# Two-layer attention and bilinear GLU on one core: two more groups' scores in block form, and every queue in a new order

## The chip, the cores and the metric

One core of one Trainium2 chip runs the whole program in one launch. The metric is the time of an execution on the device in microseconds (us), the median of several runs. Before the change it is 383.03 us, the median of three runs (381.39, 383.03, 383.17).

## The reference

Input x has 2048 tokens of 448 values. Two layers alternate, A (attention with a dilated local window) and B (a gated product without a nonlinearity), each with a layer norm ahead and a residual, and the pair runs twice with the same weights:

```python
def _A_ref(x, wqkv, wo):          # H = 16 heads of Dh = 28; W, dil = 8, 2
    q, k, v = split(x @ wqkv)
    idx = pos[:, None] - (jnp.arange(8) * 2)[None, :]     # 8 keys: 0, 2, .. 14 back
    logits = einsum("bhsd,bhswd->bhsw", q, k[idx]) * Dh ** -0.5, -1e9 where idx < 0
    o = einsum("bhsw,bhswd->bhsd", softmax(logits), v[idx])
    return o @ wo

def _B_ref(x, w_gate, w_up, w_down):                      # F = 1792
    return ((x @ w_gate) * (x @ w_up)) @ w_down

x = x + _A_ref(_layernorm(x), wqkv, wo)
x = x + _B_ref(_layernorm(x), w_gate, w_up, w_down)
# and both once more
```

## The kernel before

**Stages.** The program calls the four layers 0 to 3 (0 and 2 attention, 1 and 3 GLU). Tokens are cut into chunks (`ACH`, `BCH`, lines 54 and 55): layer 0 into 256, 512, 512, 512, 256, so that chunk 4 is tokens 1792 to 2047. `SEQ` (line 67) interleaves chunks of different layers: A00 A01 B10 A02 B11 and so on. A block is 128 tokens.

**Layer norm and transposes.** `ln_chunk` (line 619) makes statistics and the normalized rows of a block on DVE (line 650) and turns them: for the first 14 blocks of layer 0 on PE (line 660, copied out at 668), for all others with a DMA transpose in SP's queue (line 653), into `xnTa` for layers 0 and 2 and `xnTb` for 1 and 3.

**Attention.** `qk_chunk` (line 745) makes K and Q of a chunk, four units of four heads, evicted to `qk` at line 778. `v_group` (line 800) makes V. Queries are handled in groups of two blocks of 120 (group 0 has one block of 128), 9 groups in a layer. A block of 120 queries and 128 keys is cut into two halves c of 64 queries and 64 keys. There are two forms of scores:

- the old form in `attn_front` (line 894): for each head a matmul of 28 rows (head dimension) by 64 keys by 64 queries, 64 of them for a group (line 908), four PSUM banks, then exponential (915) and mask `MK` (925);
- the block form in `attn_front2` (line 933): two heads share 64 rows, and K is copied into `KB` with the other head's rows set to zero, four masked copies for a group (lines 957, 958, on POOL, DVE or ACT by the order), so that one matmul of 64 rows by 128 columns gives both heads; 16 of them for each c (line 965), two banks, exponential (971), mask `MB` (980). V's halves then stand swapped for half of the heads, so that V is evicted in three pieces (`new_way` in `v_group`, line 867) where the old form has one (888) beside the piece for the last four heads (844).

`new_way` chooses: the block form for layer 2 and for groups from `G0` = 4 on in layer 0. `KB` lies in columns of `qk` that hold no K at that time (`kb_col`, line 730; layer 0 puts it over the keys of early tokens and waits for all of their readers, `old_readers`). `attn_back` (986) multiplies with V (line 998, "AV": 64 small matmuls for a group), `norm` divides by the sums, and `y_blocks` (1048) makes the output projection Y of two blocks, added to x at 1061.

**GLU.** `b_chunk` (1071) makes gate and up of 128 features in one unit of 14 matmuls (G), evicts gate on ACT (1097), multiplies on DVE (1100) into `hT[:, fc, hs, :]`, where hs alternates with the chunk, and then multiplies with w_down (Dd). The first chunk uses hs = 0, the second hs = 1; before that parts of `hT` hold staged weights and masks: `MT2`, from which `MB` is made, is in `hT[:, 10, 1]`, a zero tile for warm-up matmuls in `hT[:, 13, 1]`.

**Order.** Each operation is added to a list and has a number; nothing is ordered at run time. `ORD` (line 59) writes out, engine by engine, the order of all numbers, and `BANK` the PSUM banks of each PE operation. Both come from a planner that is not in the file, with assumed durations. `a+b@24.40` in PE's order interleaves a burst of small matmuls a with steps of a large operation b, cut into strips of 32 columns (line 371); b is then a's host. Each engine works its list strictly in order and waits on semaphores for what an operation needs; SP's list holds nearly all DMAs, so that a DMA that waits holds up those behind it. Weight loads wait in SP's queue for an earlier weight's landing (`link`).

Of the kernel before, what the change touches and what calls it, by code (L numbers as in the profile page):

```python
# [44 lines left out]
G0 = 4  # L45
# [14 lines left out]
    "pe": "72!v 73 74 75 76 77 78 79 80 81 82 83 138!v 142!v 84 85 86 87 88 89 227!a 229 228!p 231!o 230!p 232!p 233 161!v 239!d 158!a 234!p 240!p 164!v 268!a 167!a 269!p 260!a 243!a 261!p 262!a 256!a 191!a 263!p 258!a 257!p 206!v 259!p 182!a 188!a 185!v 248!v 276!a 370!a 368!v 212!a 371!p 215!a 369!p 374!v 586!d 209!a 375!p 281!v 584!a 587 585!p 588!a 582!v 272!a 583!p 589 273!p 372!v 293!v 373!p 387!a 289!a 388!p 290!p 396!a 511!a 298!v 513!a 512!p 514!p 509!a 415!o 401!a 420!a 510!p 515!a 391!v 516!p 392!p 528!a 306!v 529!p 329!d 307!p 540!a 323!v 326!v 545!a 335!v 320!v 341!a 332!v 347!a 353!a 338!v 409!a 344!a 548+410@23.25.40!v 601!a 350!v 359!v 602!p 356!a 362!d 423!v 363!v 562!a 533!v 364!p 534!p 365 567!a 458!d 464!v 455!a 556!a 431!v 618!v 557!p 432!p 570+467~4@24.40!av 461!v 479!a 473!a 613!v 485!v 470!a 476!a 482!v 488!a 494!v 491!v 497!a 640!v 635!a 498!v 606!a 499!p 500 578!v 503 579!p 504 607 621+505@24.40.40!p 506 675!a 643+681~4@24.40!vv 678!v 772!d 751!v 773!p 752!p 749!a 755!v 750!p 629!a 753!a 630!p 754!p 756 690!a 768!a 687!a 651!v 769!p 652!p 684!a 702!v 779!a 696!v 693!v 699!a 708!v 714!a 802!o 711!a 784!v 705!a 717!a 723!a 718!v 787!d 797 719!p 720 805+724~2@24.40.40!-v 837!v 725!p 726 846!v 843!v 840!v 917!d 915!a 918!p 911!v 913!v 916!p 914!p 930!a 912 931!p 935!a 813!v 936!p 814!p 942!v 849 969!a 852!v 964!v 858!a 855!a 861!a 947!v 870!v 864!a 873!v 867!a 950+876@24.40!a 997!d 879!a 1003!v 972+880~2@24.40!va 1000!a 881!p 882 885!v 994!v 886 1015!v 1012!v 887!p 1009!v 1006 888 958!v 1024 1018!v 959!p 1122!v 1126!v 1123!p 1127!p 1141!v 1146 980!a 1142!p 981!p 1147 1124!a 1030!v 1125!p 1128!v 1021!a 1058!v 1129!p 1052!a 1027!v 1055!a 1033!v 1153!a 1061!v 1064!a 1067!a 1070!a 1036!a 1079!v 1073!v 1076!a 1037 1082!a 1158!a 1038!p 1180!v 1091!a 1039 1088 1085!a 1094!a 1161+1224~1@24.40!vd 1215!v 1095 1175!v 1096!p 1097 1183+1218~1@24.40!vv 1221!v 1329!v 1169!v 1299!v 1170!p 1300!p 1297!a 1293!v 1312!v 1295!a 1298!p 1313!p 1294 1296!p 1317!v 1191!a 1318!p 1236!v 1192!p 1334!o 1227!a 1230!v 1356!o 1233!v 1239!v 1248!a 1351!o 1242!v 1245!v 1254!a 1378!v 1251!v 1337+1265@24.24.40.40!v 1322!v 1266 1373!a 1323!p 1267!p 1257!v 1359+1258@24.40!v 1345!v 1259!p 1346!p 1381+1260~3@24.40!-v 1268 1413!v 1422!v 1419!a 1416!v 1367!v 1425!v 1368!p 1428!v 1389!a 1434!v 1390!p 1440!v 1437!v 1431!v 1452!a 1449!a 1446!v 1443!v 1463!a 1497!d 1455!v 1509!v 1464 1456 1465!p 1491!v 1466 1457!p 1500!a 1503!v 1512 1458 1521!a 1494!v 1559!a 1524!a 1562!v 1515!v 1574!a 1506!v 1527!a 1571!a 1518!v 1565!a 1530!a 1583!v 1568 1577 1580!v 1595!a 1533!v 1586!a 1592!v 1534 1541!a 1535!p 1542 1589!v 1543!p 1598!v 1536 1544 1601!v 1607 1604!v",  # L60
    "act": "2 3 14 131 132 135 136 140 144 149 235 150 236 155 237 156 162 159 238 165 168 241 179 242 270 180 271 245 244 173 266 197 221 174 198 222 192 267 264 265 186 203 204 278 277 377 376 379 282 592 253 254 286 287 274 275 294 378 295 389 390 397 398 314 300 315 299 518 519 416 303 304 421 520 393 406 330 541 324 327 546 336 407 342 439 321 348 440 354 333 339 345 549 351 550 360 445 446 357 603 425 563 428 553 429 554 459 568 465 456 619 571 462 572 468 659 733 734 480 660 474 665 666 614 575 486 477 471 483 495 489 492 641 636 576 739 740 608 623 622 676 644 682 645 821 626 679 627 758 774 648 649 757 759 760 782 827 822 828 895 691 688 685 703 697 780 700 896 694 709 803 988 712 715 785 706 798 806 901 902 989 838 847 792 844 841 1106 1107 810 811 793 922 920 932 943 970 965 850 859 853 856 862 948 1046 865 1047 871 874 951 868 877 952 998 1004 974 1001 1112 995 1016 1113 1013 955 956 1010 1007 1025 977 1019 978 1130 1132 1148 1031 1131 1199 1205 1200 1022 1059 1277 1206 1133 1053 1278 1028 1056 1034 1154 1062 1065 1068 1071 1080 1074 1077 1083 1159 1092 1181 1089 1086 1283 1284 1225 1176 1216 1166 1167 1184 1185 1219 1330 1222 1188 1304 1189 1314 1301 1332 1397 1319 1335 1237 1228 1398 1231 1357 1403 1404 1234 1240 1352 1372 1243 1249 1246 1255 1252 1379 1338 1342 1343 1374 1361 1360 1364 1382 1414 1365 1475 1386 1476 1423 1420 1387 1417 1426 1429 1435 1481 1482 1441 1432 1438 1447 1450 1453 1444 1553 1554 1498 1510 1492 1504 1501 1522 1513 1495 1525 1560 1516 1563 1575 1507 1528 1572 1519 1566 1531 1569 1578 1584 1596 1581 1593 1587 1599 1590 1606",
# [36 lines left out]
def n_grp():  # L98
    return 9 if PAIRED else NQB
# [304 lines left out]
def build(nc, A_x, A_wqkv, A_wo, B_w_gate, B_w_up, B_w_down, out):  # L404
# [325 lines left out]
    def kb_col(li, g):  # L730
        return (HALF if li else 0) + 512 * (g % 2)
# [9 lines left out]
    def block_readers(a, z):  # L741

        return [("S2", 0, g, c) for g in range(G0, n_grp()) if kb_col(0, g) < z and kb_col(0, g) + 512 > a for c in range(2)]

# [55 lines left out]
    def v_group(li, qbs, prio):  # L800
# [32 lines left out]
        if plain:  # L833
            while n == 2 and rpos["v2"] % NV2 == NV2 - 1:
                rpos["v2"] += 1
            r2 = [ring("v2", ("AV", li, q)) for q in qbs]
            t0 = [r[0] for r in r2]
            assert n == 1 or t0[1] == t0[0] + 1
            v2slot.update({(li, q): t for q, t in zip(qbs, t0)})
            def fp(E):  # L840
                dst = v2_sb[0:nk, t0[0]:t0[0] + n, :].rearrange("p s (h e) -> p s h e", e=32)[:, :, :, 0:DH]
                src = ps[0:nk, bk[1]:bk[1] + 1, VD - nv:D - nv] if split else ps[0:nk, bk[0]:bk[0] + 2, VD:D]
                src = src.rearrange("p s (h e) -> p s h e", e=DH)
                return E.activation(dst, src, ACT.Copy) if hasattr(E, "activation") else E.tensor_copy(dst, src)
            sc.add(("act", "dve"), one(fp, [("VT", li, q) for q in qbs]), {"act": act_est(n * (D - VD)), "dve": dve_est(n * (D - VD))},
                   deps=list(keys) + ["c_v2"] + [r[1] for r in r2], prio=prio)
# [396 lines left out]
```

## Time and profile before

| | |
|---|---|
| median of three runs | 383.03 us |
| the profiled execution | 384.27 us |
| its span, first to last instruction | 382.5 us |
| granted TensorE clock | 1.00 |
| masked copies of K (lines 957, 958) | 3 on ACT, 4 on DVE, 51 on POOL |
| old scores, matmuls (line 908) | 224 |
| block scores, matmuls (line 965) | 432 |

In profile lines PE is the matrix engine, PEld its weight loads (beside the matmuls), DVE the vector engine, ACT the scalar engine, POOL GpSimd, SP the engine whose queue issues DMAs (SPq). A line such as `29.73 0.50 PE L368 ... x6 [1.82 <-DMA a<-b]` gives the start, the length, engine and source line, and in brackets the idle time before and what ended it. Most matmuls go through one helper, so they all have line 368, and tiles tell them apart: `xnTa,WQK` K and Q, `WV,xnTa` V, `wo_g,oT` Y, `xnTb,WGU` gate and up, `WD,hT` the down product. A timeline row that stands for one instruction ends when its result is out; the next starts earlier, so that lengths overlap and the distance of starts is the cost.

### The profile page before, as it was taken

The page shows a single profiled execution, that of the slowest core. Times are in us where ns is not written, and L with a number is a line of the kernel's source. Part 1 is how long each engine was busy: PE and PEld are TensorE (multiplying, and loading weights), DVE is VectorE, ACT ScalarE, POOL GpSimd, SP SyncE. Part 2 cuts the span into 40 slices and gives each one's busy share as a digit, 9 for nine tenths or more (in the row PEclk, how much of TensorE's full clock was granted, in tenths as well). Part 3 has the DMA queues.
Part 4 walks back from the last instruction along what each step waited for, and adds up shares of the span by engine and source line. Part 5 has one row for each costly group of instructions (what it writes and reads, how often), then busy time and mean ns, then how long its engine had stood idle before and what let it go on. Part 6 is the DMA issues. An engine that isn't in the chain of part 4 may idle for free.

```text
span 382.5 us, 13285 instructions
## 1 busy us (share of the span) xinstructions
PE 373.5 (98%) x5902; PEld 211.3 (55%) x5902; DVE 277.1 (72%) x571; ACT 201.6 (53%) x373; POOL 94.3 (25%) x120
## 2 busy tenths in 40 slices
PE   8978999999999999999999999999999999999997
PEld 4536568544455545545566577655455444445754
DVE  6976899989677686788858865786968887335414
ACT  4977996737536934266534484376645524124310
POOL 8710779180000260007200039002900000000000
PEclk9999999999999999999999999999999999999999
DMA  8855364800521053101314006210233013301002
GB/s 271 217 105 147 79 112 113 107 7 14 73 53 31 0 83 64 25 14 22 69 24 70 2 12 116 29 31 9 21 76 52 3 25 73 74 26 38 2 2 84
DMA packets 55100, 22.69 MB, mean 59 GB/s; under 512 B 46132, under 2 KB 54148, under 8 KB 55044
## 3 DMA queue, kind: packets, MB, share of 16 engines
q1 hardware_dynamic: 54612, 21.34, 27.7%
q8 instruction: 46, 0.75, 0.8%
q10 hardware_dynamic: 432, 0.52, 0.4%
q14 instruction: 10, 0.08, 0.1%
HBM read 8.54 MB, written 2.71 MB: 29 GB/s over the span
## 4 chain that ended last, share of the span: by engine, by line
PE 91%; DMA 4%; DVE 3%; SPq 0%; ACT 0%; issue 0%
PE ps L368 84%; PE ps L998 2%; PE ps L965 2%; PE ps L371 2%; DMA xnTa<-xn_sb 1%; PE ps L1112 1%; DMA xnTb<-xn_sb 1%; DMA x_sb<-in_A_x_dram 1%; DVE xn_sb L650 1%; DVE st L629 0%; SPq L467 0%; PE ps L908 0%; DVE R_sb L1022 0%; DVE O_sb L1008 0%; PE ps L660 0%
## 5 line engine op out<-in xcount | busy, mean ns | idle before, releaser
L368 PE MATMUL ps<-xnTb,WGU 64*128 64x512 bf16 (+1 forms) x1940 | 177.7, 333 | 1.1 <-DMA xnTb<-xn_sb 1.1
L368 PEld LDWEIGHTS ps<-xnTb,WGU 64*128 64x128 bf16 x1940 | 94.2, 94 | 71.3 <-DMA xnTb<-xn_sb 1.2
L958 POOL TENSOR_SCALAR qk<-qk,pm 128x512 bf16<-128x512 bf16 (+1 forms) x51 | 76.6, 1521 | 179.1 <-ACT qk L778 105.7
L1097 ACT ACTIVATE g_sb<-ps 128x512 bf16<-128x512 f32 (+1 forms) x140 | 69.2, 509 | 95.9 <-PE ps L368 89.1
L1100 DVE TENSOR_TENSOR hT<-g_sb,ps 128x512 bf16<-128x512 bf16 (+1 forms) x140 | 76.9, 572 | 53.3 <-ACT g_sb L1097 53.0
L368 PE MATMUL ps<-WD,hT 64*128 64x448 bf16 x808 | 83.7, 349 | 0.0
L368 PEld LDWEIGHTS ps<-WD,hT 64*128 64x128 bf16 x808 | 38.5, 94 | 33.1 <-ACT g_sb L1097 0.2
L368 PE MATMUL ps<-xnTa,WQK 64*128 64x512 bf16 (+1 forms) x504 | 53.9, 353 | 2.0 <-DMA xnTa<-xn_sb 1.8
L1061 DVE TENSOR_TENSOR x_sb<-x_sb,ps 128x448 bf16<-128x448 bf16 x62 | 36.4, 615 | 16.8 <-PE ps L368 16.4
L629 DVE BATCH_NORM_STATS2 st<-x_sb 128x6 f32<-128x448 bf16 x64 | 38.7, 615 | 2.0 <-DMA x_sb<-in_A_x_dram 1.5
L650 DVE TENSOR_SCALAR xn_sb<-x_sb,mv,rstd 128x896 bf16<-128x896 bf16 (+1 forms) x64 | 35.1, 572 | 3.2 <-ACT rstd L634 1.8
L971 ACT ACTIVATE E_sb<-ps 128x1024 bf16<-128x1024 f32 (+1 forms) x28 | 27.7, 993 | 15.7 <-PE ps L965 15.0
L368 PEld LDWEIGHTS ps<-xnTa,WQK 64*128 64x128 bf16 x504 | 23.6, 94 | 22.4 <-issue 2.8
L778 ACT ACTIVATE qk<-ps 128x1024 bf16<-128x1024 f32 (+1 forms) x28 | 26.0, 947 | 7.2 <-PE ps L368 7.2
L368 PE MATMUL ps<-wo_g,oT 64*128 64x448 bf16 x250 | 28.7, 349 | 0.0
L368 PE MATMUL ps<-WV,xnTa 64*128 64x336 bf16 (+3 forms) x252 | 23.7, 304 | 0.0
L980 DVE TENSOR_TENSOR E_sb<-E_sb,MB 128x1024 bf16<-128x1024 bf16 (+2 forms) x30 | 18.7, 631 | 5.1 <-ACT E_sb L971 5.0
L632 ACT ACTIVATE lnv<-mv,eps_sb 128x2 f32<-128x2 f32 (+1 forms) x33 | 9.4, 295 | 24.0 <-DVE mv L631 24.0
L1022 DVE STREAM_SHUFFLE R_sb<-O_sb 128x960 f32<-128x960 f32 (+1 forms) x18 | 21.1, 1179 | 0.0
L1043 DVE TENSOR_TENSOR oT<-O_sb,R_sb 128x960 bf16<-128x960 f32 (+1 forms) x16 | 17.3, 1091 | 4.8 <-ACT R_sb L1024 4.7
L1023 ACT ACTIVATE R_sb<-R_sb 128x960 f32<-128x960 f32 (+1 forms) x18 | 17.1, 958 | 3.7 <-DVE R_sb L1022 3.6
L1008 ACT ACTIVATE O_sb<-ps 128x512 f32<-128x512 f32 (+1 forms) x22 | 12.2, 571 | 12.7 <-PE ps L998 12.5
(63 smaller groups left out, 239.3 us busy)
## 6 DMA issues: line engine op xcount, KB each, us to landing
out_dram<-x_sb SPq DMA_DIRECT2D x15, 112.0 KB, 1.8
WGU<-in_B_w_gate_dram SPq DMA_DIRECT2D x7, 224.0 KB, 4.4
WGU<-in_B_w_up_dram SPq DMA_DIRECT2D x7, 224.0 KB, 3.9
x_sb<-in_A_x_dram SPq DMA_DIRECT2D x3, 448.0 KB, 5.8
WD<-in_B_w_down_dram SPq DMA_DIRECT2D x2, 448.0 KB, 4.2
vt<-qk SPq DMA_DIRECT2D x42, 16.0 KB
WD<-in_B_w_down_dram SPq DMA_DIRECT2D x2, 336.0 KB, 3.5
xnTb<-xn_sb SPq DMA_TRANSPOSE x32, 3.2
```

Of the source, the lines that this page charges most:

```text
L368: return lambda E: E.matmul(out(), lhs(), rhs(), start=start, stop=stop)
L629: sc.add("dve", one(lambda E, B=B: E.bn_stats(st6[:, B, :], x_sb[:, B, :]), ("bn", li, B)), 525.0, deps=[("x", li - 1, B)] + ([("xn", li - ...
L650: sc.add("dve", one(lambda E, B=B, dst=dst, src=src: E.tensor_scalar(dst, src, mv[:, B, 0:1], rstd[:, B:B + 1], ALU.subtract, ALU.mult), ( ...
L778: return E.activation(dst, src, ACT.Copy) if hasattr(E, "activation") else E.tensor_copy(dst, src)
L958: return E.tensor_scalar(dst, src, pm[:, t:t + 1], None, ALU.mult)
L971: return E.activation(E_sb[:, slot, 2 * c:2 * c + 2, 0:w], ps[:, bk[0]:bk[0] + 2, 0:w], ACT.Exp, scale=SCALE)
L980: return E.tensor_tensor(e, e, m, ALU.mult)
L1022: sc.add("dve", one(lambda E: E.stream_shuffle(R_sb[:, rs, 0:w], O_sb[:, op, 0:w], [DH] * 32), ("Rs", li, g)), dve_est(w) + 100.0, deps=[( ...
L1043: return E.tensor_tensor(oT[:, :, t:t + n].rearrange("p h (d n) -> p h d n", d=nd), O, R, ALU.mult)
L1061: sc.add("dve", one(lambda E: E.tensor_tensor(x_sb[:, B, :], x_sb[:, B, :], ps[:, bk[w], 0:D], ALU.add), ("x", li, B)), dve_est(D), deps=[ ...
L1097: sc.add("act", one(lambda E, gs=gs, bk=bk: E.activation(g_sb[:, gs, 0:nt], ps[:, bk[0], 0:nt], ACT.Copy), ("G", li, j, fc)), act_est(nt), ...
L1100: sc.add("dve", one(lambda E, gs=gs, bk=bk, fc=fc: E.tensor_tensor(hT[:, fc, hs, 0:nt], g_sb[:, gs, 0:nt], ps[:, bk[1], 0:nt], ALU.mult), ...
```

## The change

Groups 2 and 3 of layer 0 get their scores in block form. Their `KB` lies in columns of `hT` with hs = 1 that nothing uses before the second GLU chunk (features 4 to 7 for group 2, 10 to 13 for group 3). Group 3 waits for the masks and the last warm-up matmul, and the products of the second GLU chunk for the scores. V in block form is now two operations, so that its odd part and its two even parts may run on different engines.

```diff
-G0 = 4
+G0 = 2
+GK = 4
...
     def kb_col(li, g):
-        return (HALF if li else 0) + 512 * (g % 2)
+        return (HALF if li else 0) + 512 * (g % 2) if li or g >= GK else None
+
+    def kb_view(li, g):
+        a = kb_col(li, g)
+        v = hT[:, 4 + 6 * (g % 2):8 + 6 * (g % 2), 1, :] if a is None else qk[:, 0, :, a:a + 512]
+        return v.rearrange("p h (d c n) -> p h d c n", d=2, c=2)
...
+            war = list(keys) + [p for _, p in slots] + ["c_v"]
+            sc.add(("act", "dve"), one(odd, ("Vo", li, qbs[0])), {"act": act_est(n * 112), "dve": dve_est(n * 112)}, deps=war + [("VT", li, q) for q in qbs if plain], prio=prio)
+            sc.add(("act", "dve"), [(lambda E: even(E, 0), None), (lambda E: even(E, 64), [("V", li, q) for q in qbs])], {"act": 2 * act_est(n * 224) + 120.0, "dve": 2 * dve_est(n * 224)},
+                   deps=war + [("Vo", li, qbs[0])] + [("VT", li, q) for q in qbs if plain], release=[(bk, 0), (bk, 1)], prio=prio)
...
-            sc.add(("act", "dve"), [(odd, None), (lambda E: even(E, 0), None), (lambda E: even(E, 64), [("V", li, q) for q in qbs])],
-                   {"act": sum(act_est(n * x) for x in (112, 224, 224)) + 2 * 130.0, "dve": sum(dve_est(n * x) for x in (112, 224, 224))},
...
-        KB = qk[:, 0, :, kb_col(li, g):kb_col(li, g) + 512].rearrange("p h (d c n) -> p h d c n", d=2, c=2)
+        KB = kb_view(li, g)
...
-            war = [("S2", li, g - 2, c)] if g - 2 >= (0 if li else G0) else old_readers(kb_col(li, g), kb_col(li, g) + 512)
+            if g - 2 >= (0 if li else max(G0, GK) if g >= GK else G0):
+                war = [("S2", li, g - 2, c)]
+            elif li == 0 and g < GK:
+                war = MBD + [("warm", WARM + FILL - 1)] if g % 2 else []
+            else:
+                war = old_readers(kb_col(li, g), kb_col(li, g) + 512)
```

`ORD` and `BANK` are new for all engines and all of the program. Numbers shift, since 26 operations are added. In names, PE's order in the two places that the prediction speaks of (QK c.u is unit u of chunk c, "1st" and "2nd" its two halves, T a block's transpose on PE, G f unit f of the chunk named):

| | before | after |
|---|---|---|
| from the scores of group 1 on | QK 2.1 1st, QK 2.0 1st, T 12, QK 2.1 2nd, T 13, QK 2.0 2nd, QK 2.3 1st, **QK 4.2 1st**, T 11, QK 2.3 2nd, AV 1, QK 4.1 1st | QK 2.1 1st, QK 2.3 1st, T 11, QK 2.1 2nd, QK 2.0 1st, QK 2.3 2nd, T 12, QK 2.0 2nd, T 13, AV 1, **QK 4.3 1st**, QK 4.0 1st |
| from Y of blocks 4, 5 to the first unit of layer 1's chunk 1 | AV 5 with Y 4,5 as host, V 13,14 1st, G 10, G 13, V 2nd, G 12, Dd, AV 4, Dd, scores, V 11,12, Dd, V, Dd, scores, **G 1** | Y 4,5, AV 5, G 13, V 13,14 1st, G 12, G 10, V 2nd, AV 4, Dd, Dd, V 11,12, scores, Dd, scores, V, Dd, Y 6,7 1st, **G 1** |

In SP's order the transposes of blocks 14 and 15 of layer 0 were ahead of and behind two loads of w_up and are now next to each other ahead of the loads that follow; the packed writes of K and Q of chunk 4 (`vt<-qk`) were spread to behind the first transposes of layer 1's chunk 1 and are now, but for one, ahead of the transposes of chunk 0; the four transposes of layer 1's chunk 1 had other DMAs between them and now stand together. On DVE, block 15's normalized rows are made behind 55 operations in place of 56, two of them copies of PE transposes that ACT made before. The masked copies of group 2 are given to DVE (two) and POOL (two), those of group 3 to ACT (two), DVE and POOL; V of group 2 to DVE, of group 3 to ACT; V of group 4 moves from ACT to DVE, of group 5 from DVE to ACT. AV of groups 5 of layer 0 and 2 of layer 2 lose their hosts, AV of the last two groups of layer 0 share one.

## What the time will do, and why

> **What bounds the kernel now.** I read the page's busy times first, then the waits of PE alone, then the windows by stage.
>
> ```profile
> PE 373.5 (98%) x5902; PEld 211.3 (55%) x5902; DVE 277.1 (72%) x571; ACT 201.6 (53%) x373; POOL 94.3 (25%) x120
> ```
> ```profile
> PE ps L368 <- DMA xnTa<-xn_sb: 1.8, 1, 1.8
> PE ps L908 <- issue: 1.3, 1, 1.3
> ...
> PE ps L368 <- DMA xnTb<-xn_sb: 1.1, 1, 1.1
> ```
> ```profile
> 38.00:48.00 10.00, 9.99 (x296) 5.48 (x292) 8.37 (x17) 9.42 (x15) 6.81 (x5) 1.00 0.35 76
> 48.00:64.00 16.00, 15.97 (x315) 11.88 (x316) 15.78 (x32) 12.82 (x24) 13.36 (x9) 1.00 0.52 110
> ...
> 77.00:374.50 297.50, 297.50 (x4349) 163.73 (x4346) 209.06 (x411) 143.06 (x264) 51.57 (x36) 1.00 0.20 37
> ```
>
> In a window row the columns after the length are the busy time of PE, of its weight loads, of DVE, ACT and POOL. The reader is to see three things. From 77 to 374.5 us PE is busy in all of the 297.5 us, so nothing that a new order does there can gain except by fewer PE instructions. Of PE's waits behind the start-up only three are over 0.3 us: 1.8 us for a transpose into xnTa, 1.3 us that nothing in the profile releases, 1.1 us for a transpose into xnTb; together 4.2 us, 1.1% of the span, and all before 77 us. And in that early part two other engines are nearly as full as PE: ACT 9.42 of 10 us from 38 to 48, DVE 15.78 of 16 us from 48 to 64. So the stretch before 77 us is bound by three engines at once, and that is where this change adds work to two of them.
>
> **The first wait.** The PE timeline around it, SP's queue, DVE's rows (the last normalized block, the second mask of group 1, a PSUM copy), and the chain of waits:
>
> ```profile
> 29.73 0.50 PE L368 MATMUL ps<-xnTa,WQK 64*128 64x256 bf16 x6 [1.82 <-DMA xnTa<-xn_sb]
> 30.05 0.29 PE L660 MATMUL ps<-hT,xn_sb 64*128 64x64 bf16 x8
> 30.17 1.04 PE L368 MATMUL ps<-xnTa,WQK 64*128 64x512 bf16 x8
> 31.14 0.68 PE L998 MATMUL ps<-E_sb,v_sb 64*32 64x64 bf16 x64
> ```
> ```profile
> 22.91 1.12 SPq L467 DMA_DIRECT2D WGU<-in_B_w_up_dram  x2
> 24.07 1.28 SPq L653 DMA_TRANSPOSE xnTa<-xn_sb  x1
> ```
> ```profile
> 21.43 0.40 DVE L650 TENSOR_SCALAR xn_sb<-x_sb,mv,rstd 128x512 bf16<-128x512 bf16 x1
> ...
> 27.11 0.68 DVE L925 TENSOR_TENSOR E_sb<-E_sb,MK 128x1024 bf16<-128x1024 bf16 x1
> ...
> 30.39 0.42 DVE L668 COPY xnTa<-ps 128x512 bf16<-128x512 bf16 x1 [2.60 <-PE ps L660]
> ```
> ```profile
> 24.07 5.52 DMA xnTa<-xn_sb
> ...
> 72.16 4.56 DMA xnTb<-xn_sb
> ```
>
> Before, block 15 is normalized at 21.83 us, but its transpose stands behind two weight loads in SP's queue and is issued only at 24.07; it lands 5.52 us later, at 29.59. PE wants it from 27.91, at the first piece of chunk 4 (tokens 1792 to 2047). The new order does two things. In SP's queue the transposes of blocks 14 and 15 stand together, ahead of those two loads. DVE takes on two PSUM copies and one normalization ahead of block 15 (0.4 us each) and puts two statistics with their sums behind it; I put its end at 22.2 us, an issue at 22.3 and, with the same 5.52 us, a landing at 27.8. In PE's queue three things now stand ahead of the first piece of chunk 4 that stood behind it: the PE transpose of block 11 (30.05 to 30.17, 0.12), the rest of one K/Q unit (30.17 to 31.14, 0.97) and the AV of group 1 (31.14 to 31.76, 0.62). That is 1.71 us of cover, so PE asks at 27.91 + 1.71 = 29.6 for what lands between 27.8 and 29.6. I take **-1.8 us** here; the bounds are 0 (the landing slips by as much again) and -1.82. What is covered must itself be ready: the AV needs the second mask of group 1, which DVE finished at 27.8 before, now about the same, over a microsecond ahead of its place.
>
> **The second wait.**
>
> ```profile
> 76.77 1.47 PE L368 MATMUL ps<-xnTb,WGU 64*128 64x512 bf16 x12 [1.08 <-DMA xnTb<-xn_sb]
> ```
> ```profile
> 66.88 1.24 SPq L798 DMA_TRANSPOSE v_sb<-vt  x1
> 68.17 0.82 SPq L787 DMA_DIRECT2D vt<-qk  x2
> 69.03 4.43 SPq L653 DMA_TRANSPOSE xnTb<-xn_sb  x3
> ```
> ```profile
> 64.85 1.15 DVE L1061 TENSOR_TENSOR x_sb<-x_sb,ps 128x448 bf16<-128x448 bf16 x2 [0.33 <-PE ps L368]
> ...
> 68.11 0.41 DVE L1100 TENSOR_TENSOR hT<-g_sb,ps 128x256 bf16<-128x256 bf16 x1
> ...
> 69.42 0.73 DVE L650 TENSOR_SCALAR xn_sb<-x_sb,mv,rstd 128x896 bf16<-128x896 bf16 x1
> ```
> ```profile
> 38.64 0.92 PE L368 MATMUL ps<-wo_g,oT 64*128 64x448 bf16 x8
> 39.40 0.92 PE L368 MATMUL ps<-WV,xnTa 64*128 64x448 bf16 x8
> ```
>
> Three transposes of chunk 1 go out in a row from 69.03, one every 1.48 us; the last starts near 72.0 and lands 4.56 us after 72.16. The first of them stands behind a transpose of v and two packed writes (66.88 to 69.03). In the new queue these writes stand far earlier, so blocks 2 and 3 go out ahead of the rush and only 4 and 5 remain. On DVE two more of the products for hT stand ahead of blocks 4 and 5 (0.41 us each), so block 5 comes at about the same distance behind its output projection or 0.9 us later. On PE the first half of the next Y (38.64 to 39.40, 0.76 us) and the AV of group 5, no longer interleaved, stand between that projection and the first unit of chunk 1: 1.3 us more cover. I take **-1.1 us**, bounds 0 and -1.08.
>
> **The scores of groups 2 and 3.** The chain of waits prices both forms, and the next AV:
>
> ```profile
> 36.63 0.64 PE ps L908 x64
> ...
> 41.08 0.75 PE ps L908 x64
> ...
> 42.58 0.61 PE ps L998 x64
> ...
> 54.46 0.23 PE ps L965 x16
> ```
>
> Old: 0.64 + 0.75 = 1.39 us. New: four block scores at 0.23 = 0.92. **-0.5 us** on PE. AV keeps its 64 matmuls; two AVs lose their interleaving with a host matmul, one pair shares a host: +0.3, bounds 0 and +0.6 (an AV alone is 0.61).
> The Trainium skill, TensorEngine Tiling (Array Packing), Tiling Modes and Theoretical Speedup, speaks against this part: four row tiles of 32 rows are to give twice what two of 64 give, so that 28-row scores would cost half of the block form, not more. By it this part would be 0.92 - 0.46 = +0.5 us; the rows above show the opposite sign, and the sum goes by them.
>
> **What the block form adds elsewhere.** Per group four masked copies of K, eight in all: three on POOL, three on DVE, two on ACT. V of these groups is evicted in three pieces in place of one, for group 2 on DVE, which did not have it before, for group 3 on ACT.
>
> ```profile
> L958 POOL TENSOR_SCALAR qk<-qk,pm 128x512 bf16<-128x512 bf16 (+1 forms) x51 | 76.6, 1521 | 179.1 <-ACT qk L778 105.7 <-DVE qk L778 60.9 <-PE ps L965 11.6
> ...
> L888 ACT ACTIVATE v_sb<-ps 128x672 bf16<-128x672 f32 x3 | 2.2, 730 | 0.1
> ...
> L957 ACT ACTIVATE qk<-qk,pm 128x512 bf16<-128x512 bf16 (+1 forms) x3 | 1.9, 647 | 0.6 <-DVE qk L778 0.5
> L958 DVE TENSOR_SCALAR qk<-qk,pm 128x512 bf16<-128x512 bf16 x4 | 1.9, 542 | 0.0
> ```
> ```profile
> 74.20 1.66 DVE L867 CAST v_sb<-ps 128x224 bf16<-128x224 f32 x3 [0.57 <-PE ps L368]
> ```
> ```profile
> 68.42 1.45 ACT L867 ACTIVATE v_sb<-ps 128x224 bf16<-128x224 f32 x3
> ```
>
> Copies: 2 x 0.65 + 3 x 0.54 = 2.9 us. V: 1.66 + 1.45 - 2 x 0.73 = 1.65. Together 4.6 us more on ACT and DVE, of which two DVE copies (1.1) fall in the 2.60 us in which DVE idles beside the first wait (its row at 30.39) and hide there. The other 3.5 us fall between 32 and 48, where ACT and DVE together have 0.58 + 1.63 = 2.2 us free in the quoted ten. Walking the two queues by hand, each bank that PE asks for comes within some tenths of its time, and three or four are late by 0.1 to 0.4: the units of chunk 3 behind the exponentials of group 3, and the v units behind the exponential of group 4. I put **+0.8 us** on PE, bounds 0 and +3.5. POOL is clear of it: its copies start at the same K/Q eviction as before, three more at 1.52 us each, and its last for group 4 is done about a microsecond before PE asks.
>
> **The stall inside the scores of group 1.**
>
> ```profile
> 21.68 0.47 PE L908 MATMUL ps<-qk 28*64 28x64 bf16 x36 [0.27 <-ACT qk L778]
> 23.49 0.32 PE L908 MATMUL ps<-qk 28*64 28x64 bf16 x28 [1.34 <-issue]
> ```
> ```profile
> q8 instruction: 1, 0.02, 2.1%
> ```
>
> PE stops in the middle of one operation with nothing to wait for, and the only instruction transfer of 20 to 24 us lies there (the DMA view of that window): I read it as a code block that came late behind weight traffic. The instructions ahead of this point are the same in kind and number in the new order, so I keep it: 0, bounds -1.3 and +0.5.
>
> **The sum.** The profiled execution took 384.27 us, 382.5 of span and 1.77 around it. -1.8 - 1.1 - 0.5 + 0.3 + 0.8 = -2.3, which gives 382.0. That execution is slower than all three runs: 1.24 us above their median (383.03) and 2.9 above the fastest (381.39), which is just what the two transpose waits cost. Either the profiler costs the 1.24, then the new median is 383.03 - 2.3 = 380.7; or waits on landings differ from run to run and the median already lacks part of them, then it is 382.0. I take 381.0, three parts of the first to one of the second.
>
> **Rivals.**
> (a) *ACT and DVE take over between 32 and 64 us.* For it: their windows above are 94 and 99% full. All 4.6 us would come up on PE; from 3.4 us up (1.8 + 1.1 + 0.5) the change loses. With the waits gone: 384.27 - 3.4 + 0.3 + 4.6 = 385.8; and since a late DVE also makes the last xnTb transpose late, up to 386.9. Against it: DVE idles in the stretch before 32 us, and PE itself is served in time with 0.03 us lost from 48 to 64 now.
> (b) *The landings move with the issues.* The 5.52 us of the first transpose lie in weight traffic, and the loads pushed behind it meet it in flight; PE then waits as before and only the scores pay: 384.27 - 0.5 + 0.3 + 0.4 = 384.5 on the profiled basis, 383.2 on the median's. Against it: 1.7 us of cover on PE don't depend on the landing.
> (c) *The code block comes in time too*, since fewer small matmuls and another DMA order surround it: a further -1.3, 379.7. Against it: the same instructions lead up to the same place. The Trainium skill, Runtime: NRT & Kernel Launch, Instruction fetch mechanics, calls the crossing of a code block mostly hidden; by it the 1.34 us would not be the block's and (c) falls away, though the row shows a stop that nothing else accounts for.
> (d) *The new order leaves a bank or a transpose late after 77 us*, where there is no slack to lose from. Each wait of the size of the two above costs 1 to 2 us: 382.0 to 383.0. Nothing in the trace of before speaks for it, as its stages there have DVE at 70% and ACT at 48%.
>
> **Chances.** Forecast 0.42, at 381.0 with its own range 380.0 to 382.0; (a) 0.18, (b) 0.17, (c) 0.10, (d) 0.13. What a measurement of this kernel can tell from no change is about 0.5%, 1.9 us: below 381.1 is faster, above 384.9 slower. The forecast lies across the first line, a little over half of it below: 0.25; with all of (c), 0.10, and a third of (b) and (d) together, 0.10, in which less than the whole mishap strikes, faster is 0.45. Slower is most of (a) and a little of (d), 0.17. Same is the rest, 0.38. The range 379.0 to 385.3 leaves out the better half of (c) and the worse half of (a).
>
> **What would show it.** Right: PE's two waits for xnTa and xnTb are gone or under 0.3 us, the last xnTa transpose is issued near 22 us, the old scores shrink from 224 to 96 matmuls and the block scores grow from 432 to 496, and PE has gaps of a few tenths between 38 and 48 us released by ACT or DVE. The 1.3 us of "issue" stays in the scores of group 1. Wrong: PE waits of over 3 us in total between 32 and 64 us (a), a transpose wait still over 1 us (b), or PE busy clearly under the length of a window after 77 us (d).

## The result, and the profile after

| | before | after |
|---|---|---|
| median of the runs | 382.36 us (8 runs, 381.39 to 383.75) | 380.3 us (8 runs, 379.25 to 381.37) |
| ratio, 95% interval | | 0.994 [0.9918, 0.9963] |
| the profiled execution, and its span | 384.27, 382.5 us | 379.54, 377.8 us |
| PE idle within the span | 6.5 us | 2.3 us |
| of it: issue stall, first, second transpose wait | 1.34, 1.82, 1.08 us | 0, 0, 0 |

Run again later, the kernel after gave 379.72 us, a ratio of 0.9933 [0.9907, 0.9958]. The change gains about 2 us, 0.6%. The two profiled executions differ by more, 4.74 us of span, and the difference can be added up: 4.14 us less idle time of PE, 0.77 us less PE work, 0.17 us more behind the last matmul. The 4.14 are the three stalls of the kernel before (4.24), all gone, and 0.1 of small waits that are new.

These are all of the waits of PE that the profile of the kernel after lists (us in total, times, longest):

```profile
PE ps L555 <- DVE eps_sb L508: 1.2, 1, 1.2
PE ps L915 <- ACT qk L785: 0.3, 1, 0.3
PE ps L369 <- POOL WQK L565: 0.2, 1, 0.2
PE ps L1010 <- DVE xnTa L669: 0.2, 1, 0.2
PE ps L1010 <- DMA v_sb<-vt: 0.2, 1, 0.2
```

The first is the start-up, which was there before. Of the rest none is over 0.3 us. (The later run's profile has one of 0.66 us, for normalized rows at 6.2 us, and otherwise none over 0.3 behind the start-up.) The windows of the same execution (after the length: PE, its weight loads, DVE, ACT, POOL):

```profile
38.00:48.00 10.00, 10.00 (x276) 5.79 (x272) 9.90 (x20) 9.93 (x15) 5.36 (x4) 1.00 0.68 163
48.00:64.00 16.00, 15.82 (x338) 13.03 (x334) 15.92 (x37) 11.91 (x28) 16.00 (x11) 1.00 0.57 103
...
77.00:369.80 292.80, 292.80 (x4277) 169.58 (x4274) 204.87 (x403) 141.21 (x265) 45.44 (x31) 1.00 0.22 37
```

From 38 to 48 us DVE went from 8.37 to 9.90 of 10 and ACT from 9.42 to 9.93, and PE still lost nothing: three engines at 99% and more, side by side. (At the same time after the start the kernel after is about 3 us further on in its work.) Behind 77 us PE is busy throughout, as before. The idle time that went lies wholly ahead of 77 us.

The transposes of blocks 14 and 15 in SP's queue, and the block scores of groups 2 and 3 with what follows them on PE:

```profile
20.52 2.65 SPq L654 DMA_TRANSPOSE xnTa<-xn_sb  x2
```
```profile
31.73 0.40 PE L977 MATMUL ps<-qk,hT 64*128 64x64 bf16 x16
31.97 1.03 PE L369 MATMUL ps<-xnTa,WQK 64*128 64x512 bf16 x8
...
33.40 0.40 PE L977 MATMUL ps<-qk,hT 64*128 64x64 bf16 x16
33.64 1.50 PE L369 MATMUL ps<-WV,xnTa 64*128 64x448 bf16 x14
...
37.89 0.40 PE L977 MATMUL ps<-qk,hT 64*128 64x64 bf16 x16
38.12 1.03 PE L369 MATMUL ps<-xnTa,WQK 64*128 64x512 bf16 x8
...
38.99 0.40 PE L977 MATMUL ps<-qk,hT 64*128 64x64 bf16 x16
39.32 0.68 PE L1010 MATMUL ps<-E_sb,v_sb 64*32 64x64 bf16 x64
```

Two transposes in 2.65 us, so the second goes out at about 22 us, in place of 24.07. The four bursts cost the distances 0.24, 0.24, 0.23 and 0.33, together 1.04 us (the printed 0.40 runs until the results are out).

### The profile page after: what moved, and what is told of

Read it like the earlier page. It is cut to its first block, busy times and chain, and to the rows that moved or that the text cites. A ratio compares the mean times of both kernels' runs of the same rounds, so it can differ in the third digit from the quotient of the medians.

```text
span 377.8 us, 13091 instructions
## 1 busy us (share of the span) xinstructions
PE 372.8 (99%) x5796; PEld 220.7 (58%) x5796; DVE 277.2 (73%) x571; ACT 203.9 (54%) x382; POOL 100.3 (27%) x123
## 4 chain that ended last, share of the span: by engine, by line
PE 90%; DMA 3%; DVE 3%; SPq 2%; ACT 1%; POOL 0%; issue 0%
PE ps L369 83%; PE ps L1010 2%; PE ps L977 2%; PE ps L1124 1%; PE ps L372 1%; DMA x_sb<-in_A_x_dram 1%; DMA v_sb<-vt 1%; SPq L794 1%; SPq L805 1%; DVE st L630 1%; DMA vt<-qk 1%; ACT E_sb L983 1%; POOL WQK L575 0%; SPq L468 0%; DVE xn_sb L651 0%; PE ps L661 0%
## 5 line engine op out<-in xcount | busy, mean ns | idle before, releaser
L369 PEld LDWEIGHTS ps<-xnTb,WGU 64*128 64x128 bf16 x1928 | 99.5, 94 | 63.4 <-ACT g_sb L1109 0.3
L970 POOL TENSOR_SCALAR qk<-qk,pm 128x512 bf16<-128x512 bf16 (+1 forms) x51 | 77.9, 1544 | 159.2 <-DVE qk L785 64.5
L369 PE MATMUL ps<-WD,hT 64*128 64x448 bf16 x828 | 85.9, 349 | 0.0
L369 PEld LDWEIGHTS ps<-WD,hT 64*128 64x128 bf16 x828 | 40.0, 94 | 34.5 <-ACT g_sb L1109 0.2
L983 ACT ACTIVATE E_sb<-ps 128x1024 bf16<-128x1024 f32 (+1 forms) x32 | 31.7, 996 | 9.6 <-PE ps L977 9.6
L369 PEld LDWEIGHTS ps<-xnTa,WQK 64*128 64x128 bf16 x504 | 25.1, 94 | 18.8 <-POOL WQK L565 0.4
L369 PE MATMUL ps<-wo_g,oT 64*128 64x448 bf16 x256 | 29.8, 349 | 0.0
L785 ACT ACTIVATE qk<-ps 128x1024 bf16<-128x1024 f32 (+1 forms) x27 | 25.0, 941 | 5.8 <-PE ps L369 5.7
L992 DVE TENSOR_TENSOR E_sb<-E_sb,MB 128x1024 bf16<-128x1024 bf16 (+2 forms) x34 | 21.2, 634 | 0.4 <-ACT E_sb L983 0.3
L369 PEld LDWEIGHTS ps<-wo_g,oT 64*128 64x128 bf16 x256 | 13.5, 94 | 10.1 <-issue 0.2
```

Of the source, the lines that this page charges most:

```text
L369: return lambda E: E.matmul(out(), lhs(), rhs(), start=start, stop=stop)
L970: return E.tensor_scalar(dst, src, pm[:, t:t + 1], None, ALU.mult)
L983: return E.activation(E_sb[:, slot, 2 * c:2 * c + 2, 0:w], ps[:, bk[0]:bk[0] + 2, 0:w], ACT.Exp, scale=SCALE)
L992: return E.tensor_tensor(e, e, m, ALU.mult)
```

## The experiments

Twelve runs. All are compared with the kernel before on the same chip; in a diff of an order, numbers are those of the order, with their names behind.

**Three moves, each alone and together.** The numbers of operations up to 276 are the same in both kernels, so parts of the new order can be put into the old kernel. `b_sp` takes over the new order of SP's first 27 DMAs:

```diff
 sp:
-0 .. 12 107 110 13 109 111 112 113 108 106 114 224 117 115 226 118 116 119 ..
+0 .. 12 106 110 109 107 108 13 112 111 115 113 114 224 226 118 117 116 119 ..
   (224, 226: blocks 14 and 15 of layer 0; 106 to 118: weights)
```

> The kernel before with only the first 27 DMAs of SP in the order of the kernel after (blocks 14 and 15 turned one behind the other, other order of the early weight loads); every other queue as before. Theory (the early loads decide both the stall inside the scores of group 1 and the landing of block 15): the 1.34 us issue stall is under 0.3, block 15 is issued near 22 us and lands near 27.5, PE asks for it at 27.91 - 1.34 = 26.6, so a wait of about 1 us stays there; together -2 us against before. Rival (the code block's stall has nothing to do with the loads): the stall stays at 1.3, PE asks at 27.9, the wait is under 0.3; -1.5 to -1.8 us. Rival (landings move with issues): both stay, within 0.5 us of before.

`b_pe` gives the first wait its cover on PE, and nothing else:

```diff
 pe:
-374!v 586!d 209!a 375!p 281!v 584!a
+374!v 209!a 375!p 281!v 586!d 584!a   (586: QK 4.2 1st; 209, 375, 281: T 11, QK 2.3 2nd, AV 1)
```

> The kernel before with one move in PE's order: the first half of QK 4.2 stands behind T 11, the rest of QK 2.3 and AV 1 in place of ahead of them. Theory: 1.7 us of cover take the first transpose wait from 1.82 to under 0.3; the 1.34 us issue stall stays; -1.5 to -1.8 us. Rival (the three pieces put ahead are not ready, or what followed them now waits): a wait of over 1 us appears beside the moved pieces, within 0.5 us of before.

`b_sp2` puts layer 1's four transposes together:

```diff
 sp:
-450 537 597 599 448 452 454   (450, 448, 452, 454: layer 1's blocks 2 to 5)
+450 448 452 454 537 597 599   (537: v; 597, 599: packed writes)
```

> The kernel before with one move in SP's order: the transpose of v and two packed writes that stand between the first and the other transposes of layer 1's chunk 1 go behind all four. Theory: the last xnTb transpose lands 2 us earlier, the second wait (1.08) is gone, -1.1 us. Rival (what is moved back is late in its place): the AV of the last groups of layer 0 waits for v instead, 0 or worse.

`b_all` makes all three moves.

> The three moves together, still with the old form of scores for groups 2 and 3. Theory (the kernel after gains by the order alone, the block form is worth nothing): all three stalls under 0.3 us, -4.2 us in the profile, the median as fast as the kernel after (380.3) or faster. Rival (the block form carries part of the gain): about 0.5 us or more slower than the kernel after, with PE busy 0.8 us longer than there.

And to see what such waits do from run to run, both kernels unchanged, and `b_sp` once more:

> The kernel before unchanged. Theory (its three stalls vary from run to run, since each hangs on when a DMA among the weight loads gets through): their sum is clearly below 4.2 us, 1.5 to 3.5, and the median difference to the kernel after is near 2 us because of that. Rival (the stalls are fixed): 1.3, 1.8 and 1.1 again, and the 2 us in the median have another cause.

> The kernel after unchanged, to see which of its waits recur. Theory (the order has cover for the waits that vary): none over 0.3 us behind the start-up, issue stall under 0.3, span within 1.5 us of 377.8. Rival (the profile shown was a lucky one): one of the issue stall or the two transpose waits is back with over 0.5 us.

> b_sp once more, since its times fall into two groups (379.9 to 381.4, and 384.0 to 384.8 with a mean granted clock of 0.996 in most of the second). Theory (without PE's cover a late landing of block 15 becomes one wait of over 2 us, and such a wait also costs the clock for some microseconds, as the 3.87 us wait of c_blk did): an execution of the second group shows one wait of 2 to 3.5 us for xnTa at about 26 us and a granted clock near 0.5 behind it. Rival (the second group has nothing to do with waits): its clock is low with no wait of over 1 us ahead of it. If the profile falls into the first group, this stays open.

Measured, with the three stalls in each profiled execution:

| | median, range (us) | ratio to before | issue stall | first wait | second wait |
|---|---|---|---|---|---|
| before, first profile | | | 1.34 | 1.82 | 1.08 |
| before2 | 381.88, 380.77 to 384.89 | 1.0 [0.9976, 1.0023] | 0 | 0.40 | 0.95 |
| b_sp | 382.68, 379.9 to 384.81 | 1.0017 [0.9988, 1.0045] | 0 | 0.23 | 0 |
| b_sp_again | 381.05, 379.97 to 385.37 | 0.9991 [0.9947, 1.0034] | 0 | 0.59 | 1.19 |
| b_pe | 382.12, 380.77 to 383.59 | 0.9993 [0.9975, 1.0012] | 0.79 | 0 | 0.91 |
| b_sp2 | 381.7, 380.46 to 383.24 | 0.9985 [0.9965, 1.0005] | 0 | 1.07 | 0.24 |
| b_all | 380.26, 380.08 to 380.57 | 0.9955 [0.9939, 0.9972] | 0 | 0 | 0 |
| after2 | 379.72, 379.33 to 380.25 | 0.9933 [0.9907, 0.9958] | 0 | 0 | 0 |

The issue stall is the one inside the scores of group 1; `b_pe` has a second, of 0.53 us, at 18.26 us.

The whole list of waits of `before2`, the very kernel whose first profile showed 1.3, 1.8 and 1.1:

```profile
PE ps L554 <- DVE eps_sb L507: 1.2, 1, 1.2
PE ps L368 <- DMA xnTb<-xn_sb: 0.9, 1, 0.9
PE ps L660 <- DVE xn_sb L650: 0.6, 2, 0.3
PE ps L368 <- DMA xnTa<-xn_sb: 0.4, 1, 0.4
PE ps L660 <- DVE pm L507: 0.4, 1, 0.4
PE ps L908 <- ACT qk L778: 0.3, 1, 0.3
PE ps L368 <- POOL WQK L564: 0.2, 1, 0.2
```

and that of `b_all`, where only the start-up is left:

```profile
PE ps L554 <- DVE eps_sb L507: 1.2, 1, 1.2
```

What follows. The three stalls are not fixed costs: the same kernel lost 4.24 us to them in one execution and 1.35 in another, and its two profiled spans are 382.5 and 379.0. For the first wait SP's queue shows where the difference begins. The same DMAs in the same order, which went out at 22.91 and 24.07 us in the first profile, went out earlier in `before2`, and block 15 landed at 26.48 us in place of 29.59:

```profile
20.98 1.18 SPq L467 DMA_DIRECT2D WGU<-in_B_w_up_dram  x2
22.20 1.28 SPq L653 DMA_TRANSPOSE xnTa<-xn_sb  x1
```

Over all profiles of this case, the variants further down among them, two of the moves show their effect on their wait. Without PE's cover the first wait is between 0.23 and 1.82 us in five profiles and 0 in one (`b_t15`, below); with it, 0 in all eight. With the four transposes apart the second wait is between 0.91 and 1.19 us in four profiles and 0 in two (`b_sp` and `b_t15`); with them together, 0.24 once (`b_sp2`) and 0 in the seven others. The move of `b_sp`, the earlier issue, left 0.23 and 0.59 us of the first wait.

In the times none of the moves alone can be told from no change: the gains of 2, 1.5 to 1.8 and 1.1 us that were expected of them did not come. A part of the reason stands in the profiles: the stalls differ from run to run, and where one wait is gone another can be last (`b_sp2` has 0.3 us for a load of WD). Together the moves are worth 1.7 us, 0.45% [0.28, 0.61], and the six times lie within 0.5 us, where those of the kernel before beside them lie within 2.5. Whether the scatter goes with the waits is not shown: the kernel after, without the stalls in both its profiles, lies within 2.1 us in its first set of runs and within 0.9 in the second.

So the old form of scores in the old order, with three moves, comes to within 0.5 us of the kernel after (380.26 against 379.72 and 380.3); the intervals of the ratios overlap, and no gain of the block form can be told from these two. A gain of some tenths is not excluded: the profiled span of `b_all` is 378.5 us, those of the kernel after 377.8 and 377.7.

**One more move in SP's queue.** Which part of the new order of loads matters:

```diff
 sp:
-114 224 117 115 226 118 116
+114 224 226 117 115 118 116   (224, 226: blocks 14 and 15)
```

> The kernel before with one move in SP's order: block 15's transpose ahead of the two loads of w_up that stand between the transposes of blocks 14 and 15; the order of the early weight loads as before. Theory (the stall inside the scores of group 1 is an instruction fetch that waits behind weight packets, and takes 2.7 to 2.8 us from its start to the next matmul): the fetch starts at 19 to 21 us as in the runs with the loads' old order, not at 17.9 to 18.6 as with the new one, and what is left of the stall follows from it (start + 2.75 us less the time at which PE reaches the place). Rival (the place of block 15's transpose decides): the fetch starts before 18.7 and there is no stall.

381.26 us, 0.9989 [0.9967, 1.0011]. The instruction fetch started at 18.17 us, with no stall, which the rival had said. But `before2`, with neither move, has its fetch at 18.14. With the old order of the loads the fetch started at 20.69, 21.19, 19.30, 18.14 and 18.17 in five profiles; with the new order of `b_sp` it started between 17.86 and 18.60 in seven (an eighth, `a_old`, has 19.78, behind a stall of 1.28 us at the boundary before, as the 21.19 of `b_pe` stands behind one of 0.53). So my reading, that the new order of loads brings the fetch forward, is not shown: an early fetch comes without it. Whether it keeps late ones away stays open. With block 15 out early there was no first wait here, without any cover on PE; instead a load of WD was 0.8 us late:

```profile
PE ps L554 <- DVE eps_sb L507: 1.2, 1, 1.2
PE ps L368 <- DMA WD<-in_B_w_down_dram: 0.8, 1, 0.8
PE ps L908 <- ACT qk L778: 0.3, 1, 0.3
PE ps L660 <- DVE xn_sb L650: 0.2, 1, 0.2
```

**The block form, from both sides.** `a_old` is the kernel after with groups 2 and 3 in the old form:

```diff
-G0 = 2
+G0 = 4
 pe, in names:
-QK 2.2 1st, scores 2 (c=0), QK 2.2 2nd, V 3,4 1st, scores 2 (c=1) ... scores 3 (c=0), QK 3.1 2nd, scores 3 (c=1), AV 2
+QK 2.2 1st,                 QK 2.2 2nd, V 3,4 1st, scores 2       ...                 QK 3.1 2nd, scores 3,       AV 2
 act, dve, pool: masked copies of groups 2 and 3 out, V in one piece
 banks: of both bursts together (2: 6,7,4,5; 3: 0,1,6,7)
```

> The kernel after with groups 2 and 3 in the old form: one burst of 64 matmuls of 28 rows in place of the two bursts of 16 of each group, no masked copies for them, V in one piece; all else in the order of the kernel after. Theory of the prediction's sum (the block form is worth 0.5 us on PE and its copies cost nothing): PE busy about 0.5 us longer, 0.3 to 0.8 us slower than the kernel after. Rival (old and block form cost PE the same, since the 0.64 and 0.75 us of the chain contain more than the distance between starts): within 0.3 us of the kernel after. Rival (copies and V pieces hold PE up): faster than the kernel after by 0.3 us or more.

`c_blk` goes the other way: `b_all` with these two groups in block form, `c_blk2` the same with V and copies given to the engines in another way:

```diff
-G0 = 4
+G0 = 2
 pe:
-scores 2, QK 2.2 2nd ... scores 3, QK 3.1 1st, AV 2
+scores 2 (c=0), QK 2.2 2nd, scores 2 (c=1) ... scores 3 (c=0), QK 3.1 1st, scores 3 (c=1), AV 2
 c_blk, V 3,4:  DVE, its even pieces behind mask 2 (c=1); copies of group 3: ACT 2, DVE 1, POOL 1
 c_blk2, V 3,4: DVE ahead of the normalization of group 1, even pieces ACT; copies of group 3: DVE 3, POOL 1
 c_blk2, act:   QK 2.2 ahead of the first exponential of group 2
```

> The kernel b_all (order of before with the three moves) with groups 2 and 3 in block form: two bursts of 16 in place of the burst of 64, the second one operation later; the masked copies and V pieces on the engines that the kernel after gives them, right behind what they need; nothing else moved. Theory of the prediction's sum (PE gains 0.5 us, the extra work on ACT and DVE costs 0.8): 0 to 0.6 us slower than b_all (380.26), with some new waits of 0.1 to 0.4 us between 30 and 48 us. Rival (the copies hide, the scores pay): 0.3 to 0.8 us faster than b_all, no wait there over 0.1 us, and then as fast as the kernel after (379.7). Rival (the old order has no room for the copies): over 1 us slower than b_all.

> As c_blk, but with V of blocks 3 and 4 in time: its last-heads piece and odd piece on DVE ahead of the normalization of group 1, its even pieces on ACT as in b_all, all of group 3's masked copies but one on DVE, and ACT's eviction of QK 2.2 ahead of the first exponential of group 2. Theory (the block form itself is worth a few tenths on PE and what it needs is only that V and copies come in time): the 3.87 us wait is under 0.6, the clock stays at 1.0, and the time is within 0.6 us of b_all (380.26). Rival (the old order has no room for the block form): waits of over 1.5 us in total between 30 and 48 us, 382 or more.

| | median (us) | ratio to before | PE from AV 1 to AV 3 (us, in the profile) |
|---|---|---|---|
| after2 (new order, block form) | 379.72 | 0.9933 [0.9907, 0.9958] | 27.57 to 44.12: 16.55 |
| a_old (new order, old form) | 384.04 | 1.0048 [1.0029, 1.0066] | 28.95 to 48.43: 19.48 |
| b_all (old order, old form) | 380.26 | 0.9955 [0.9939, 0.9972] | 27.81 to 43.82: 16.01 |
| c_blk2 (old order, block form) | 384.17 | 1.0063 [1.0049, 1.0078] | 27.86 to 45.76: 17.90 |
| c_blk (old order, block form) | 388.55 | 1.0176 [1.014, 1.0212] | 27.98 to 50.23: 22.25 |

(The two orders have not quite the same work between these AVs, so compare the first two rows with each other and the last three.) The scores themselves are as the rows of before said. In `a_old`:

```profile
35.05 0.71 PE L915 MATMUL ps<-qk 28*64 28x64 bf16 x64
35.68 0.93 PE L369 MATMUL ps<-WV,xnTa 64*128 64x448 bf16 x8
37.02 0.74 PE L369 MATMUL ps<-WV,xnTa 64*128 64x448 bf16 x6 [0.41 <-ACT E_sb L922]
38.02 0.93 PE L369 MATMUL ps<-wo_g,oT 64*128 64x448 bf16 x8 [0.26 <-DVE v_sb L851]
...
42.14 0.81 PE L915 MATMUL ps<-qk 28*64 28x64 bf16 x64
42.88 0.74 PE L1010 MATMUL ps<-E_sb,v_sb 64*32 64x64 bf16 x64
44.16 0.82 PE L369 MATMUL ps<-xnTa,WQK 64*128 64x512 bf16 x6 [0.53 <-ACT E_sb L922]
```

Two bursts at 0.63 and 0.74, 1.37 us, against 1.04: the block form saves PE 0.33 us. The rest of the 2.9 us by which `a_old` is longer here is not scores. Three waits, 1.20 us together, are for banks that an exponential or V holds; as I read it, the old form's exponentials stand behind all 64 matmuls, and this order has no other work there. The remaining 1.4 us are PE rows that run longer. A part of that are stops too short to show as idle time, since a row runs on until its result is out: in the row of 14 K and Q matmuls at 40.29 us two steps lie 0.44 us apart in place of 0.22. `c_blk2` pays the other way round, with 1.31 us for a bank that an exponential holds and 0.98 for V in three pieces, against no wait in `b_all`:

```profile
PE ps L369 <- issue: 1.5, 1, 1.5
PE ps L369 <- ACT E_sb L983: 1.3, 1, 1.3
...
PE ps L369 <- ACT v_sb L856: 1.0, 1, 1.0
```

Both mixtures are slower by far more than the scores are worth in either direction, so what the order around a form does for it outweighs the form. The 0.3 to 0.8 us that were expected of `a_old` missed its 4.3 by far; for `c_blk` and `c_blk2` the rival held, that the old order has no room. The other part of the loss of `a_old` and `c_blk2` is an issue stall, below.

**A wait of 3.87 us and the clock.** `c_blk` made V late by my own placing. PE, then the windows (the first number behind the busy times is the granted clock):

```profile
34.74 0.40 PE L977 MATMUL ps<-qk,hT 64*128 64x64 bf16 x16
39.00 1.30 PE L369 MATMUL ps<-WV,xnTa 64*128 64x448 bf16 x6 [3.87 <-DVE v_sb L856]
40.09 1.70 PE L369 MATMUL ps<-wo_g,oT 64*128 64x448 bf16 x8
41.59 1.70 PE L369 MATMUL ps<-WV,xnTa 64*128 64x448 bf16 x8
43.08 1.45 PE L369 MATMUL ps<-wo_g,oT 64*128 64x448 bf16 x8
44.37 0.40 PE L977 MATMUL ps<-qk,hT 64*128 64x64 bf16 x16
```
```profile
36.50:37.00 0.50, 0.00 (x0) 0.00 (x0) 0.50 (x3) 0.50 (x2) 0.50 (x1) 1.00 0.06 12
37.00:37.50 0.50, 0.00 (x0) 0.00 (x0) 0.50 (x2) 0.50 (x2) 0.50 (x1) 0.82 0.14 25
37.50:38.00 0.50, 0.00 (x0) 0.00 (x0) 0.47 (x2) 0.50 (x2) 0.50 (x2) 0.50 0.22 25
...
43.50:44.00 0.50, 0.50 (x6) 0.26 (x4) 0.00 (x0) 0.47 (x2) 0.32 (x1) 0.50 0.00 0
44.00:44.50 0.50, 0.50 (x16) 0.23 (x12) 0.00 (x0) 0.47 (x2) 0.00 (x0) 0.86 0.00 0
```

The same work in `b_all`:

```profile
35.21 0.73 PE L368 MATMUL ps<-WV,xnTa 64*128 64x448 bf16 x6
...
38.14 0.78 PE L908 MATMUL ps<-qk 28*64 28x64 bf16 x64
```

The wait is not the whole price. PE stops at 35.13 (39.00 less 3.87); by the 0.82 the clock falls at about 37.3, 2.2 us into the wait, and by the 0.86 it is back at about 44.1, 5.1 us after PE works again. In between the same eight matmuls take 1.70 us in place of 0.92. From the wait's end to the next scores PE takes 39.00 to 44.37, 5.37 us, for what `b_all` does from 35.21 to 38.14, 2.93: another 2.4 us. All six runs of `c_blk` have a mean granted clock of 0.991 or 0.996, all six of `c_blk2` one of 1.00. A wait of 1.82 us (before) left the clock at 1.00, and behind the 1.31 us of `c_blk2` such a row of eight matmuls took 0.93 us. The Trainium skill, TensorE: Matmul & The Clock Gate, Part 1: The HAM clock gate (the "warmup" mystery), has two clocks, half and full, and a fall to the half after an idle window of about 3.4 us that runs free of the kernel. Half and full agree; the 2.2 us are shorter than the window, and the measurement decides.

**The issue stall.** `a_shift` is `a_old` with nine warm-up matmuls cut into eight each:

```diff
-ins = [(matmul of 512 columns)]
+ins = [(matmul of 64 columns) x 8]   for the first nine warm-ups
```

> The kernel a_old with nine warm-up matmuls of 512 columns cut into eight of 64 each, so that 63 matmuls stand ahead of everything else and the places where PE runs into a new block of its code (each 256 instructions) lie 63 matmuls earlier. Theory (the 1.33 us stall at 113.9 us is a code block of small matmuls that PE eats in 1.8 us while the next takes 2.7 to fetch): a boundary now cuts the burst in half, the blocks beside it take over 5 us each, and the stall is gone; 1.3 us faster than a_old (384.04). Rival (the stall belongs to the two interleaved AVs themselves): the stall stays in the burst, at the same operations, and the time stays.

383.65 us, 1.0035 [1.0017, 1.0054]. In `a_old` the stall looked like this, in the middle of two AVs with a host:

```profile
113.49 0.39 PE L372 MATMUL ps<-xnTb,WGU 64*32 64x512 bf16 x3
115.22 0.37 PE L372 MATMUL ps<-xnTb,WGU 64*32 64x512 bf16 x1 [1.33 <-issue]
```
```profile
112.08:113.90 1.82, 1.80 (x145) 1.46 (x144) 1.73 (x6) 1.04 (x3) 0.00 (x0) 1.00 0.04 9
113.90:115.20 1.30, 0.00 (x0) 0.00 (x0) 0.32 (x1) 0.00 (x0) 0.00 (x0) 1.00 0.49 100
```

In `a_shift` it is gone: its burst runs from 112.07 us without a stop, and no wait of PE is listed from 100 to 120 us. The operations are the same but for the nine warm-ups; what has moved is their place in the code. The stall of 1.28 us that the profile of `a_old` has at 18.62 is gone as well, and another boundary gave a new one of 0.71 at 30.69. The medians differ by 0.4 us and not by 1.3, with intervals that overlap, so the move is shown in the profile and not in the times. Counted in the order of time in PE's list (a matmul is two, with its weight load), all eight issue stalls of over 0.5 us in the fourteen profiles lie at the same place within 256 instructions: behind 449 (twice), 705 (twice), 1217, 2497 (twice) and 4289, each 193 above a multiple of 256. Where a stall came, PE went on 2.3 to 3.0 us after the start of that block's 16 KB instruction transfer:

| | fetch starts | PE goes on | between | stall |
|---|---|---|---|---|
| before | 20.69 | 23.49 | 2.80 | 1.34 |
| b_pe | 15.57 | 18.26 | 2.69 | 0.53 |
| b_pe | 21.19 | 23.85 | 2.66 | 0.79 |
| a_old | 15.60 | 18.62 | 3.02 | 1.28 |
| a_old | 112.58 | 115.22 | 2.64 | 1.33 |
| a_shift | 29.15 | 31.40 | 2.25 | 0.71 |
| c_blk | 67.79 | 70.26 | 2.47 | 1.34 |
| c_blk2 | 63.66 | 65.99 | 2.33 | 1.53 |

So the reading of the stall as a late code block, argued in the prediction, is now shown, by its place and by moving it. It seems to have two ways to come about: the fetch starts late (before, at 20.69 us against 18.14 in `before2`; what held it up on the DMA side stays open), or the block is eaten faster than one can be fetched: in `a_old` 145 small matmuls passed in 1.82 us. The Trainium skill, Runtime: NRT & Kernel Launch, Instruction fetch mechanics, has the blocks of 256 instructions and the fetch of the next during the current one, which these places bear out; that the crossing is mostly hidden holds for most of the 46 crossings of a run, but not for the eight of the table.

**Left open.** The times of `b_sp` fall into two groups, 379.9 to 381.4 and 384.0 to 384.8, most of the second with a mean granted clock of 0.996; one of `b_sp_again` was 385.37 at 0.991. The profile of the second attempt fell into the first group. The kernel before has such runs too (384.6 and 384.89 us at 0.996); `b_all` and the kernel after have none among 21. A long wait with a halved clock behind it, as in `c_blk`, would fit, but no profile shows it.

## Why the prediction was right, and where it was not

The time (381.0 forecast, 380.3 and 379.7 measured) and the sign were right; two terms of the sum and the choice between two bases were not, and that the time came out so near is in part luck. Point by point, by the difference of the two profiles:

- **First transpose wait, -1.8.** It went whole (-1.82); the last transpose of xnTa goes out at 22, as forecast. `b_pe` has no first wait by PE's cover alone; by the earlier issue alone `b_t15` has none, but `b_sp` 0.23 and 0.59. What the term missed is that 1.82 was one draw: 0.40 in `before2`.
- **Second wait, -1.1.** Gone (-1.08). SP's order is the cause, as far as `b_sp2` and the seven other profiles with it show (at most 0.24); but this wait too was a draw, absent in two profiles of the old arrangement.
- **Scores, -0.5.** Right in sign and mechanism, -0.33 in size: the four bursts cost 1.04 in place of 0.92, as the last has 0.33 to the AV behind it. The Trainium skill, TensorEngine Tiling (Array Packing), Theoretical Speedup, which spoke against this part, gives up to 4x for 32 rows and up to 2x for 64. Here the form in tiles of 32 rows was the slower one, 1.37 against 1.04.
- **AV hosting, +0.3.** Not measured by itself. What is left of the difference when all other terms are taken off (-4.74 + 1.82 + 1.08 + 1.34 + 0.33 - 0.18) is -0.35, so nothing of a loss is to be seen.
- **Extra work on ACT and DVE, +0.8.** This term failed. The work came (ACT and DVE at 99% from 38 to 48), the waits of a few tenths did not: PE 10.00 of 10, and 0.18 us at 59.91 for a v is all. The step that failed was the walk through the two queues by hand: I followed where each bank is late, and put three or four small delays on PE that, as the busy PE shows, the new order of PE and the banks had room for. That the risk was real `c_blk2` shows, with 2.3 us of waits for an exponential and for V in an order that had no room.
- **Code block, 0.** This term failed too, inside its bounds: -1.34. "The instructions ahead of this point are the same in kind and number, so I keep it" is true, and the boundary lies at the same matmul in both kernels; but whether PE stalls there hangs on when the fetch starts, and that differs from run to run (17.86 in the profile of the kernel after). Rival (c), at 0.10, gave what the profile shows; its reason, the other DMA order, is not shown.
- **The basis.** I took the profiled 384.27 to be 1.24 us slow for the profiler's sake, three to one. It was the other reading: the profiled executions of `before2` (380.77) and of the kernel after (379.54) are no slower than their medians, the three stalls vary, and the median (382.36 over eight runs) lacked about half of what the first profile had. Two errors then cancelled: too little taken off for an execution with all three stalls (-2.3 where the profile gave -4.74), and most of that taken from the median of runs that had less to lose, which fell by 2.06.
- **Rivals.** (a) did not come: PE lost 0.18 us from 30 to 64 us; (b) not, as the landing comes about 5 us after an issue 2 us earlier; (d) not: PE is busy in all of 77 to 369.8 us.

## What to carry to other kernels

A wait on a DMA in one profile is a draw, not a price: profile the kernel twice before a stall goes into a sum at its full size. Moves against waits in a row are to be tried together, as here none alone showed in the times and all three did. And a cheaper form of an operation needs an order planned for it: put into another order by hand it cost, in its own stretch alone, more than five times what it saves on PE (1.9 us against 0.33), and in its own order no gain of it could be told from the times.

## What was not expected of the hardware

PE stopped for 0.5 to 1.5 us at eight boundaries of 256 instructions and went on 2.3 to 3.0 us after the block's transfer had started; in one of them 145 small matmuls had passed in 1.82 us just before. Where a boundary falls was moved with 63 small matmuls far ahead. And in `c_blk` an idle time of 3.87 us of PE cost 2.4 us more behind it, as the clock was granted at 0.50 for nearly 7 us; it fell 2.2 us into the wait.
